# Loads of three key and value tiles for 21 heads, rounds that read all landed tiles first, and longer weight loads, in a single-step attention and mixer kernel

## The chip, the cores and the metric

The kernel runs on one core of a Trainium2 chip. The metric is the time of one execution on the device in microseconds. The engines are named as in the profile: PE (matrix products), PEld (its weight loads), DVE (vector), ACT (activations), POOL, and SP, which here only issues the loads from memory (DMA). The core has sixteen DMA engines, and a load of 128 rows is spread over all of them.

## The reference

One decode step for 4 batch items: layer normalisation modulated by a condition vector, attention of 32 query heads over 8 cached key/value heads of 4096 positions each, an output projection with a gated residual, and a small two-layer mixer on top. All is fp32. Keys and values are 134 MB of the 157 MB that are read.

```python
mod = (silu(c) @ w_mod).reshape(4, 6, 1, 512)
sa, ca, ga, sb, cb, gb = (mod[:, e] for e in range(6))
h = layernorm(x) * (1 + ca) + sa
q = (h @ wq)                                    # 32 heads of 128
s = einsum("bhqd,bhkd->bhqk", q, repeat(k_cache, 4)) * 128 ** -0.5
o = einsum("bhqk,bhkd->bhqd", softmax(s), repeat(v_cache, 4))
x = x + ga * (o.reshape(4, 1, 4096) @ wo)
h = layernorm(x) * (1 + cb) + sb
u = gelu(einsum("bsd,sf->bdf", h, w1) + b1)      # f = 1792
x = x + gb * (einsum("bdf,fs->bds", u, w2) + b2)
```

## The kernel before, in words

The work is cut into NS = 32 heads i (batch item i // 8, key/value head i % 8). A head needs two tiles of 2 MB, its keys K_i and its values V_i, each 128 rows of 16 KB. They pass through a ring of three buffers of two tiles (96 KB of each of the 128 partitions). `load_first` brings K0 and K1 (`kk`), and each `load_pair(i)` brings K_(i+2) and V_i in one load of 4 MB with rows of 32 KB, so that the scores of a head run two rounds ahead of its values. At the start the ring holds weights: wm01 (the modulation's first two slices of `w_mod`) and the two halves of `wq`. In the round i = 1 the three slices wm24 take one ring buffer, and `mod` reads them after round 2. The output weights `wo` have a place of their own (`wo_p`, four tiles of two heads) and come in four loads of 2 MB.

The program writes out by hand the order in which each engine gets its work. A head passes these steps: `scores` (PE into s), `row_max` (DVE), `turn_max` (PE, pm), `col_max` (DVE), `spread_max` (PE, pb), `copy_max` (DVE, nm), `expo` (ACT, p and its row sums l), `turn` (DVE, transposes p in blocks), `sums` (PE, pl), `scale` (DVE), `values` (PE into pv), `copy_v` (DVE, po), `pick` (PE, pt), `copy_o` (DVE, oT), `project` (PE with wo, pa), `add_up` (DVE, acc). The loop over i from 0 to 23 runs, in one round, the scores of head i+2, the picking and projection of head i-1, and the values of head i in two halves. From i = 8 on, `Mixer` puts pieces of the mixer of the batch item before into the rounds (gelu on ACT, expansions on DVE, py on PE). Heads 24 to 31 and the last mixers follow the text `PLAN`, in which each word is a step; LP, LT, LK, LV and LW are its loads. `finish` ends the kernel.

All loads stand in one queue on SP, in program order. A load waits on SP until what is in its place has been read, and every later load waits behind it.

Lines that the prediction speaks of: L176 (pair loads), L181 (wo), L185 and L186 (wm24), L231 (scores), L291 (values), L215 (the products in mod, whose input is wm), L328, L343, L251 and L240 (pt, pa, pb, pm).

Of the kernel before, what the change touches and what calls it, by code (L numbers as in the profile page):

```python
# [15 lines left out]
REP = HQ // HKV  # L16
# [8 lines left out]
NARROW = NS - 3  # L25


@with_exitstack
def adaln_decode(ctx: ExitStack, tc: tile.TileContext, small, x, wmod, wq, kk, kv, vv, wo, out):
# [18 lines left out]
    wm01 = ring.tile([P, 2, 4, D], F32, name="wm01", tag="kv")  # L48
    nc.sync.dma_start(wm01, wmod[0])
# [3 lines left out]
    for k in range(0, 4, 2):  # L53
        t = ring.tile([P, 2, HQ * DH], F32, name=f"wq{k}", tag="kv")
        nc.sync.dma_start(t, wq[k // 2])
        wqt += [t[:, 0], t[:, 1]]
# [34 lines left out]
    wo_p = [wos.tile([P, 2, REP, D], F32, name=f"wo{h}") for h in range(0, HKV, 2)]  # L91
    wo_t = [wo_p[h // 2][:, h % 2] for h in range(HKV)]
# [64 lines left out]
    KT, VT, WM = {}, {}, {}  # L157

    def slots():
        return ring.tile([P, 2, SK], F32, name="kv", tag="kv")  # L160

    def key(t, i):
        KT[i] = t

    def value(t, i):
        VT[i] = t.rearrange("p (j d) -> p j d", d=DH)

    def load_first():
        t = slots()
        nc.sync.dma_start(t, kk)  # L170
        key(t[:, 0], 0)
        key(t[:, 1], 1)

    def load_pair(i):
        t = slots()
        nc.sync.dma_start(t, kv[i])  # L176
        key(t[:, 0], i + 2)
        value(t[:, 1], i)

    def load_wo(h):  # L180
        nc.sync.dma_start(wo_p[h // 2], wo[h // 2])  # L181

    def load_wm24():
        w = ring.tile([P, 3, 4, D], F32, name="wm24", tag="kv")
        nc.sync.dma_start(w[:, 0:2], wmod[1])  # L185
        nc.sync.dma_start(w[:, 2], wmod[2][:, 0])  # L186
        for e in range(3):
            WM[2 + e] = w[:, e]

    def load_wm5():  # L190
        t = slots().rearrange("p s (k n) -> p (s k) n", n=D)
        nc.sync.dma_start(t[:, 0:4], wmod[2][:, 1])
        WM[5] = t[:, 0:4]
        return t[:, 4:6]

    def load_key(t, i):
        nc.sync.dma_start(t, kv[i - 2][:, 0])
        key(t, i)

    def load_v(t, i, cuts):  # L200
        value(t, i)
        src = (kv[i][:, 1] if i < NS - 2 else vv[i - NS + 2]).rearrange("p (j d) -> p j d", d=DH)
        for lo, hi in zip(cuts, cuts[1:]):
            nc.sync.dma_start(VT[i][:, lo:hi], src[:, lo:hi])
# [21 lines left out]
    def scores(i):  # L226
        b, h = divmod(i, HKV)
        S[i] = s = ps_s.tile([P, 1024], F32, name=f"s{i}", tag="s")
        for n in range(2):
            for c in range(4):  # L230
                mm(s[32 * c:32 * c + 32, n * 512:(n + 1) * 512], QT[:, b, h, :],  # L231
                   KT[i][:, (n * 4 + c) * 512:(n * 4 + c + 1) * 512], start=True, stop=True)

# [51 lines left out]
    def values(i, ks):  # L285
        if ks[0] == 0:
            PV[i] = ps_v.tile([P, 4 * DH], F32, name="pv", tag="pv")
        pT = PL[i][0]
        for k in ks:
            q = k % 4  # L290
            mm(PV[i][32 * q:32 * q + 32, :], pT[:, 128 * k:128 * k + 128:4],  # L291
               VT[i][:, 4 * k:4 * k + 4, :].rearrange("p j d -> p (j d)"), start=(k < 4), stop=(k >= 4))

    def values_narrow(i, ks, pv=None):
# [5 lines left out]
        for k in ks:  # L300
            for j in range(4 * k, min(4 * k + 4, top)):
                c = j % 4
                mm(pv[32 * c:32 * c + 32, :], pT[:, j, :], VT[i][:, j, :], start=(k == 0), stop=(j + 4 >= top))  # L303

# [32 lines left out]
    def project(i, pa=None, between=None):  # L337
        b, h = divmod(i, HKV)
        oT = OT[i]
        if pa is None:  # L340
            pa = ps_m.tile([P, D], F32, name="pa", tag="m")
            for g in range(REP):
                mm(pa[32 * g:32 * g + 32, :], oT[:, g:g + 1].to_broadcast([P, 32]), wo_t[h][:, g, :],  # L343
                   start=True, stop=True)
        else:
            for g in range(REP):
                for c in range(4):
                    mm(pa[32 * c:32 * c + 32, :], oT[:, g:g + 1].to_broadcast([P, 32]),  # L348
                       wo_t[h][:, g, c * P:(c + 1) * P], start=(g == 0 and h == HKV - 2),
# [202 lines left out]
    def finish(b, pg, py, hb, wr):  # L552
        uu = ring.tile([P, 16, D], F32, name="uu", tag="kv")
# [35 lines left out]
    def fold_gate(gate, es):  # L589
        for e in es:  # L590
            w = wo_t[HKV - 2 + e // REP][:, e % REP]
# [17 lines left out]
    load_first()  # L609
    load_pair(0)  # L610
    load_wo(0)
# [3 lines left out]
    for step in (turn, sums, scale):  # L615
        step(0)
    mix = None
    for i in range(NS - HKV):
        load_pair(i + 1)
        if i in (1, 3, 5):  # L620
            load_wo(i + 1)
        if i == 1:
            load_wm24()
        scores(i + 2)
        row_max(i + 2)
        if i:
            pick(i - 1)
            copy_o(i - 1)
        turn(i + 1)
        sums(i + 1)  # L630
        scale(i + 1)
        if i:
            project(i - 1)
            add_up(i - 1)
        turn_max(i + 2)
        col_max(i + 2)
        values(i, range(4))
        spread_max(i + 2)
        copy_max(i + 2)
        expo(i + 2)  # L640
        if i and i % HKV == 0:
            mix = Mixer(i // HKV - 1)
        if mix:
            mix.inner(i % HKV)
        values(i, range(4, 8))
        copy_v(i)
        if mix:
            mix.outer(i % HKV)
        if i == 2:
            for t in range(2, 5):  # L650
# [4 lines left out]
                else:  # L655
                    nc.scalar.activation(dst, pm, AF.Copy)
        if i == NS - HKV - 2:
            gate = spread_gate()

    mix, row = Mixer(B - 2), Mixer(B - 1)
    pve = pgx = pc = ep = spare = slot = None
    gates = list(range(2 * REP))
    cuts = {NS - 1: (0, 16, 24, 28, 30, 32), NS - 2: (0, 16, 32)}
# [3 lines left out]
    x LP27 m26 S27 P24 m27 X26 X27 b26 B26 e26 x b27 v25.1 c g t26.1 l25 t26.0 B27 s28 V25 c g L25  # L669
    v26.0 v26.1 S28 x l26 f a25 L26 V26 A25 x m28 p25 LT X28 e27 c a26 P25 t27.0 A26 b28 s29 f B28 p26 e28  # L670
    LK30 t27.1 S29 P26 v27.0 m29 l27 g LK31 T t28.1 X29 LT t28.0 s30 L27 S30 b29 v27.1 B29 e29 l28 m30 V27
    LV28 L28 a27 g X30 t29.1 t29.0 l29 L29 s31 A27 LV29 b30 p27 x B30 S31 c c m31 e30 P27 X31 v28.0 f LT LV30
    b31 v28.1 B31 f e31 LV31 l30 V28 L30 t30.1 l31 L31 a28 t31.1 A28 p28 v29.0 v29.1 t30.0 f P28 V29 v30.0 a29
    v30.1 A29 LW p29 f v30.2 v30.3 t31.0 P29 g V30 Y y a30 A30 p30 E x v31.0 f v31.1 v31.2 v31.3 V31 z31 a31 I A31 j p31
# [3 lines left out]
             "l": sums, "L": scale, "V": copy_v, "a": pick, "A": copy_o, "P": add_up,  # L678
             "LP": load_pair}
# [4 lines left out]
    for step in PLAN.split():  # L684
# [19 lines left out]
        elif op == "LT":  # L704
            slot = slots()
        elif op == "LK":
            load_key(slot[:, i % 2], i)
        elif op == "LV":
            load_v(slot[:, i % 2], i, cuts.get(i, (0, 32)))
        elif op == "LW":  # L710
            spare = load_wm5()
        elif op == "x":
            mix.expand(spare if mix.n == 6 else None)
# [75 lines left out]
```

## Time and profile before

| what | value |
|---|---|
| median of 3 runs (range) | 386.48 us (386.38 to 386.49) |
| span of the profiled execution | 384.7 us |
| mean granted PE clock | 0.883 of full |
| busy: PE, DVE, ACT | 298.7, 198.2, 112.2 us |
| DMA | 157.69 MB, mean 410 GB/s |
| wait of PE at L231 for loads of kv | 37.0 us in 19 waits |

The profiled execution has a span of 384.7 us from its first to its last instruction; the median of the runs is 1.8 us above that. Busy shares are averages over stages: PE is busy for 78% of the span, yet that says nothing on what it waits for. In the rows, a matrix product of fp32 counts twice (16 for the 8 products of one head's scores), and its duration overlaps the next one's: what a group costs is read from its start to the start of the next group.

### The profile page before, as it was taken

What the parts mean: (1) busy time and instruction counts of PE and PEld (TensorE: products, weight loads), DVE (VectorE), ACT (ScalarE), POOL (GpSimd) and SP (SyncE); (2) the same over time, 40 slices, a digit from 0 to 9 for tenths busy, and PEclk for the clock granted to TensorE, in tenths of its full rate; (3) what the DMA queues carried; (4) which work ended last, traced back from release to release, by engine and by line L of the source; (5) the groups of instructions that cost most, each with busy time, mean ns of one, the idle gap of its engine ahead of it and who ended that gap; (6) DMA issues with size and microseconds to landing.
All of it is one profiled execution on the core that took longest, in us unless ns stands there. A gap on an engine that the chain in (4) does not pass through costs nothing.

```text
span 384.7 us, 5604 instructions
## 1 busy us (share of the span) xinstructions
PE 298.7 (78%) x2380; PEld 117.2 (30%) x2380; DVE 198.2 (52%) x407; ACT 112.2 (29%) x144; POOL 7.7 (2%) x33
## 2 busy tenths in 40 slices
PE   0856777866966949979877878788888887999984
PEld 0112122311323313334322222342222343333653
DVE  1130251620451424664866545557665567778757
ACT  1001111121110110212567311124575105657276
POOL 1100000000000000000000000000000000000000
PEclk9989555985695685998999998999999999999999
DMA  8999999999999999999999999999999999999930
GB/s 331 433 433 436 411 453 433 409 432 436 423 441 433 434 436 436 434 436 431 429 425 433 428 433 434 429 433 431 429 434 436 434 436 432 424 417 423 418 122 3
DMA packets 7409, 157.69 MB, mean 410 GB/s; under 512 B 964, under 2 KB 1236, under 8 KB 1496
## 3 DMA queue, kind: packets, MB, share of 16 engines
q1 hardware_dynamic: 7376, 157.33, 95.4%
q8 instruction: 18, 0.29, 0.3%
q14 instruction: 7, 0.06, 0.0%
q10 hardware_dynamic: 8, 0.00, 0.0%
HBM read 157.32 MB, written 0.01 MB: 409 GB/s over the span
## 4 chain that ended last, share of the span: by engine, by line
DMA 60%; PE 29%; DVE 7%; ACT 2%; issue 1%; POOL 0%; SPq 0%; POOLq 0%; DVEq 0%
DMA kv<-in_kv 58%; PE s L231 8%; PE pv L291 7%; PE s L122 2%; PE qs L138 2%; DVE m L236 2%; DVE p L267 2%; DMA sm<-in_small 2%; PE pa L343 2%; PE pt L328 2%; ACT uu L562 1%; PE pb L251 1%; PE pve L303 1%; PE pm L240 1%; PE pgx L348 1%
## 5 line engine op out<-in xcount | busy, mean ns | idle before, releaser
L231 PE MATMUL s<-kv,QT 128*32 128x512 f32 x512 | 75.2, 714 | 38.9 <-DMA kv<-in_kv 37.0
L236 DVE TENSOR_REDUCE m<-s 128x1 f32<-128x1024 f32 x32 | 39.2, 1224 | 96.0 <-PE s L231 95.9
L261 ACT ACTIVATE p<-s,nm 128x1024 f32<-128x1024 f32 x32 | 35.7, 1115 | 180.6 <-DVE nm L256 180.5
L291 PE MATMUL pv<-kv,p 128*32 128x512 f32 x464 | 69.8, 670 | 0.7 <-DMA kv<-in_kv 0.7
L231 PEld LDWEIGHTS s<-kv,QT 128*32 128x32 f32 x512 | 15.8, 123 | 84.0 <-DMA kv<-in_kv 52.5
L328 PEld LDWEIGHTS pt<-g,po 128*128 128x128 f32 x236 | 31.1, 205 | 27.2 <-issue 19.9
L343 PE MATMUL pa<-wo,oT 128*32 128x512 f32 x240 | 34.6, 648 | 4.6 <-DVE oT L335 4.4
L328 PE MATMUL pt<-g,po 128*128 128x4 f32 (+2 forms) x236 | 33.9, 267 | 1.5 <-DVE po L314 1.0
L267 DVE STREAM_TRANSPOSE p<-p 128x1024 f32<-128x1024 f32 x25 | 30.9, 1234 | 0.0
L314 DVE COPY po<-pv 128x512 f32<-128x512 f32 x29 | 20.0, 688 | 16.8 <-PE pv L291 16.7
L245 DVE TENSOR_REDUCE mx<-pm 1x128 f32<-1x512 f32 x32 | 21.3, 669 | 1.1 <-PE pm L240 1.1
L442 DVE TENSOR_SCALAR u<-hb,wr,sm 128x512 f32<-128x512 f32 x40 | 19.9, 541 | 1.9 <-POOL wr L437 1.0
L506 ACT ACTIVATE u<-u 128x1024 f32<-128x1024 f32 x20 | 20.4, 1051 | 1.5 <-DVE u L442 1.4
L361 DVE TENSOR_TENSOR acc<-acc,pa 128x512 f32<-128x512 f32 x26 | 17.8, 686 | 4.3 <-PE pa L343 4.2
L261 ACT ACT_TABLE_LOAD x11 | 14.1, 1283 | 20.3 <-DVE nm L256 20.2
L251 PEld LDWEIGHTS pb<-neg,mx 1*128 1x128 f32 x64 | 10.4, 202 | 28.2 <-DVE mx L245 26.5
L122 PE MATMUL s<-wm,sT 128*4 128x512 f32 x16 | 9.1, 732 | 10.6 <-DVE sT L108 10.6
L506 ACT ACT_TABLE_LOAD x13 | 16.7, 1283 | 0.2
L291 PEld LDWEIGHTS pv<-kv,p 128*32 128x32 f32 x464 | 13.4, 146 | 7.2 <-issue 3.1
L240 PE MATMUL pm<-ident,m 128*1 128x128 f32 x32 | 9.3, 289 | 7.4 <-DVE m L236 3.5
L251 PE MATMUL pb<-neg,mx 1*128 1x1 f32 x64 | 13.1, 271 | 2.1 <-DVE mx L245 2.1
L453 PE MATMUL py<-u,sm 128*32 128x512 f32 x80 | 14.4, 616 | 0.0
(158 smaller groups left out, 214.7 us busy)
## 6 DMA issues: line engine op xcount, KB each, us to landing
kv<-in_kv SPq DMA_DIRECT2D x28, 4096.0 KB, 21.9
wq<-in_wq SPq DMA_DIRECT2D x2, 4096.0 KB, 16.3
wo<-in_wo SPq DMA_DIRECT2D x4, 2048.0 KB
kv<-in_kv SPq DMA_DIRECT2D x4, 2048.0 KB, 20.3
wm<-in_wmod SPq DMA_DIRECT2D x2, 2048.0 KB, 14.8
kv<-in_kk SPq DMA_DIRECT2D x1, 4096.0 KB
kv<-in_vv SPq DMA_DIRECT2D x3, 1024.0 KB
wm<-in_wmod SPq DMA_DIRECT2D x1, 1024.0 KB
```

The source lines that it names most:

```text
L231: mm(s[32 * c:32 * c + 32, n * 512:(n + 1) * 512], QT[:, b, h, :], KT[i][:, (n * 4 + c) * 512:(n * 4 + c + 1) * 512], start=True, stop=True)
L236: dv.tensor_reduce(M[i], S[i], axis=AX.X, op=OP.max)
L245: dv.tensor_reduce(mx, M[i].rearrange("o (c r) -> o r c", c=4).unsqueeze(1).to_broadcast([1, 4, 32, 4]), axis=AX.X, op=OP.max)
L251: mm(pb, M[i].rearrange("o c r -> o (c r)"), neg1, start=True, stop=True)
L261: nc.scalar.activation(p, S[i], AF.Exp, bias=M.pop(i), accum_out=l)
L267: dv.transpose(PL[i][0], PL[i][0])
L291: mm(PV[i][32 * q:32 * q + 32, :], pT[:, 128 * k:128 * k + 128:4], VT[i][:, 4 * k:4 * k + 4, :].rearrange("p j d -> p (j d)"), start=(k < ...
L314: dv.tensor_copy(PV[i], pv)
L328: mm(pt, po[:, c * DH:(c + 1) * DH], sel.unsqueeze(1).to_broadcast([P, m, REP]), start=(c == 0), stop=(c == n - 1))
L343: mm(pa[32 * g:32 * g + 32, :], oT[:, g:g + 1].to_broadcast([P, 32]), wo_t[h][:, g, :], start=True, stop=True)
L442: dv.tensor_scalar(u[:, e, :], hb, wr[:, j:j + 1], b1[:, j:j + 1], op0=OP.mult, op1=OP.add)
L506: nc.scalar.activation(u, u, AF.Gelu_apprx_tanh)
```

## The change

The ring becomes one tile RING of six places. For heads 0 to 20 (NP = 21) the keys and values come in 14 loads of three tiles (6 MB, rows of 48 KB, tensor `kvk`), in turn K_(a+2), V_a, K_(a+3) and V_(a+1), K_(a+4), V_(a+2), for a = 0, 3, .. 18. The prediction calls them T0 to T13. Heads 21 to 27 keep pairs, the rest single tiles. `wo` becomes one tile that is loaded in two loads of 4 MB; wm01 and wm24 lie in its places for later heads (wm24 in heads 4 to 6), no longer in the ring, so kk needs to wait for nothing. `LOADS` lists all loads in order, and `advance` is called after each step that reads a tile: it issues from the front of the list as long as what lies in the place has been read, so the load words leave `PLAN`.

The rounds of heads 0 to 20 become two halves of three tiles each. `first_half(a)` runs scores, values, scores on the tiles of one triple, `second_half(a)` values, scores, values on the next, and picking, projecting and the mixer stand behind. Heads 21 to 23 have rounds of their own (`round_of`). `copy_max` goes from DVE to ACT for heads below 26.

The order of SP's queue from the first keys on, before:

```order
L170 DMA kv<-in_kk 128x8192
L176 DMA kv<-in_kv 128x8192
L181 DMA wo_128<-in_wo 128x4096
L176 DMA kv<-in_kv 128x8192 x2
L181 DMA wo_129<-in_wo 128x4096
L185 DMA wm_337<-in_wmod 128x4096
L186 DMA wm_337<-in_wmod 128x2048
L176 DMA kv<-in_kv 128x8192 x2
```

And after, with the semaphores that a load waits for (PE is a read; DMAHW is an earlier load):

```order
L210 DMA kv<-in_kk 128x8192
L210 DMA kv<-in_kvk 128x12288 [waits DMAHW4_49,DMAHW3_49,PE_49]
L192 DMA wo<-in_wo 128x8192 [waits DMAHW0_49]
L210 DMA kv<-in_kvk 128x12288 [waits DMAHW5_49,PE_49]
L192 DMA wo<-in_wm 128x6144 [waits DMAHW1_49]
L210 DMA kv<-in_kvk 128x12288 [waits DMAHW6_49,DMAHW2_49,PE_49]
L192 DMA wo<-in_wo 128x8192 [waits DMAHW1_49,PE_49]
L210 DMA kv<-in_kvk 128x12288 [waits DMAHW0_49]
```

The second `wo<-in_wo` now waits for PE (the reads of wm24 by mod) and stands ahead of the fourth triple and all that follow, where before wo waited only for an earlier load.

PE around the first run of mod, before (scores of head 4, one round, then mod, which reads wm):

```order
L231 MATMUL s_394<-kv,QT 32x512 x8
L328 MATMUL pt<-g_122,po 128x4 x4
L275 MATMUL pl<-g_122,l 128x4
L343 MATMUL pa<-wo_128,oT 32x512 x4
L240 MATMUL pm<-ident,m 1x128
L291 MATMUL pv<-kv,p 32x512 x4
L251 MATMUL pb<-neg_87,mx 128x1
L291 MATMUL pv<-kv,p 32x512 x4
L215 MATMUL pm_445<-wm_337,sT_134 32x512 x4
L221 MATMUL pc_452<-ym,g_122 32x128 x4
L215 MATMUL pm_458<-wm_337,sT_134 32x512 x4
```

And after (the second half of a = 0, then mod, whose input is now in the place of wo):

```order
L309 MATMUL pv<-kv,p 32x512 x8
L245 MATMUL s_385<-kv,QT 32x512 x8
L309 MATMUL pv<-kv,p 32x512 x8
L255 MATMUL pm<-ident,m 1x128
L350 MATMUL pt<-g_121,po 128x4 x4
L266 MATMUL pb<-neg_87,mx 128x1
L365 MATMUL pa<-wo,oT 32x512 x4
L350 MATMUL pt<-g_121,po 128x4 x4
L365 MATMUL pa<-wo,oT 32x512 x4
L293 MATMUL pl<-g_121,l 128x4
L229 MATMUL pm_449<-wo,sT_129 32x512 x4
L235 MATMUL pc_456<-ym,g_121 32x128 x4
```

The reads of all three tiles now come first, in one run, and mod stands behind the picking and projection of two heads. The first half of a = 3 shows the other kind, on PE right behind mod:

```order
L245 MATMUL s_490<-kv,QT 32x512 x8
L309 MATMUL pv<-kv,p 32x512 x8
L255 MATMUL pm<-ident,m 1x128
L245 MATMUL s_516<-kv,QT 32x512 x8
L266 MATMUL pb<-neg_87,mx 128x1
L350 MATMUL pt<-g_121,po 128x4 x4
L255 MATMUL pm<-ident,m 1x128
L365 MATMUL pa<-wo,oT 32x512 x4
L266 MATMUL pb<-neg_87,mx 128x1
L293 MATMUL pl<-g_121,l 128x4 x2
```

Two scores with a values between them; pm, the turn of the row maxima, is all that stands between the reads.

The diff, cut to its core, with the two halves in full, since they set the order:

```diff
-    ring = ctx.enter_context(tc.tile_pool(name="ring", bufs=3))
+    ring = ctx.enter_context(tc.tile_pool(name="ring", bufs=1))
...
+    RING = ring.tile([P, 6, SK], F32, name="kv")
+    wo_t = wos.tile([P, HKV, REP, D], F32, name="wo")
+    wm01, wm24 = wo_t[:, 0:2], wo_t[:, 4:7]
+    nc.sync.dma_start(wm01, wm0)
...
+    def queue():
+        q = [entry(["K0", "K1"], kk)]
+        for n in range(NT):
+            m = n // 2 * 3
+            names = [f"V{m + 1}", f"K{m + 4}", f"V{m + 2}"] if n % 2 else [f"K{m + 2}", f"V{m}", f"K{m + 3}"]
+            q.append(entry(names, kvk[n]))
...
+        q.insert(2, ("wo", "M0", wo_t[:, 0:4], wo[0]))
+        q.insert(4, ("wo", None, wm24, wm2))
+        q.insert(6, ("wo", "M2", wo_t[:, 4:8], wo[1]))
+        return q
...
+    def advance(name=None):
+        read.add(name)
+        while LOADS:
+            kind, names, *rest = LOADS[0]
+            if kind == "wo":
+                if names not in read:
+                    return
+                nc.sync.dma_start(*rest)
+            else:
+                n, p = len(names), at[0]
+                if any(h not in read for h in held[p:p + n]):
+                    return
...
     def copy_max(i):
         nm = wk.tile([P, 1], F32, name="nm")
-        dv.tensor_copy(nm, M[i])
+        if i < NS - HKV + 2:
+            nc.scalar.activation(nm, M[i], AF.Copy)
+        else:
+            dv.tensor_copy(nm, M[i])
...
+    def first_half(a):
+        do(a + 2, scores, row_max)
+        attend(a)
+        do(a + 2, turn_max, col_max)
+        scores(a + 3)
+        do(a + 2, spread_max, copy_max, expo)
+        row_max(a + 3)
+        do(a, pick, copy_o, begin)
+        do(a + 3, turn_max, col_max)
+        project(a)
+        do(a + 3, spread_max, copy_max)
+        do(a + 2, sums, scale, turn)
+        add_up(a)
+        expo(a + 3)
+        end(a)
+        do(a + 3, sums, scale, turn)
+
+    def second_half(a):
+        attend(a + 1)
+        do(a + 4, scores, row_max)
+        values8(a + 2)
+        do(a + 4, turn_max, col_max)
+        copy_v(a + 2)
+        do(a + 1, pick, copy_o, begin)
+        do(a + 4, spread_max, copy_max, expo)
+        project(a + 1)
+        do(a + 2, pick, copy_o)
+        do(a + 1, add_up, end)
+        begin(a + 2)
+        project(a + 2)
+        do(a + 4, sums, scale, turn)
+        do(a + 2, add_up, end)
...
+    for a in range(0, NP, 3):
+        first_half(a)
+        second_half(a)
+        if a == 0:
             for t in range(2, 5):
                 pm = mod(t)
...
+            advance("M2")
+    for i in range(NP, NS - HKV):
+        round_of(i)
...
-    a23 v24.0 A23 p23 t25.0 P23 F R v24.1 LP25 G s26 t25.1 M H V24 LP26 Q a24 S26 v25.0 N s27 x A24 f p24 g
+    a23 v24.0 A23 p23 t25.0 P23 F R v24.1 G s26 t25.1 M H V24 Q a24 S26 v25.0 N s27 x A24 f p24 g
...
```

`attend` is values of all eight parts and copy_v; `do` runs steps in order; `begin` and `end` are the mixer's pieces around a round. The host packs `kvk`, `wm0`, `wm2`, `wm5` and the two parts of `wo` accordingly.

More of the change, by code (lines that the diff above doesn't have):

```diff
@@ L196, in load_key @@
[L196 to L204, printed above, removed]
+    KT, VT, WM = {}, {}, {2 + e: wm24[:, e] for e in range(3)}
+    held, read = [("Q", 0), ("Q", 0), ("Q", 1), ("Q", 1), None, None], {None, ("Q", 0), ("Q", 1)}
@@ L614, in adaln_decode @@
             step(i)
[L615 to L640, printed above, removed]
-        if i and i % HKV == 0:
[L642 to L649, printed above, removed]
+    for i in range(2):
+        for step in (sums, scale, turn):
+            step(i)
```

161 lines of the change are left out of this document (94 added, 67 removed).

## The prediction

> **What bounds the kernel now.** The page is read first: the transfer rate by slices, the queue table, the chain that ended last.
>
> ```profile
> GB/s 331 433 433 436 411 453 433 409 432 436 423 441 433 434 436 436 434 436 431 429 425 433 428 433 434 429 433 431 429 434 436 434 436 432 424 417 423 418 122 3
> q1 hardware_dynamic: 7376, 157.33, 95.4%
> DMA 60%; PE 29%; DVE 7%; ACT 2%; issue 1%; POOL 0%; SPq 0%; POOLq 0%; DVEq 0%
> ```
>
> From slice 1 to slice 37 the rate lies near 430 GB/s and hardly dips, and 60% of the chain is DMA. The DMA view of the stretch 150 to 300 us and the page's table of issues tell whether the queue ever ran empty.
>
> ```profile
> q1 hardware_dynamic: 2228, 64.62, 99.9%
> kv<-in_kv SPq DMA_DIRECT2D x28, 4096.0 KB, 21.9
> SPq L176 <- PE pv L291: 186.4, 23, 12.3
> ```
>
> The queue holds 99.9% of sixteen engines there. A pair of 4096 KB takes some 9.7 us to move (4.19 MB at 433 GB/s) and lands 21.9 us after its issue: half of that time it stood queued behind another load. SP's waits for PE (third row) cost nothing, since they end long before the queue is empty. So the kernel is bound by its bytes, and a change can win only through the rate, the head or the tail; it loses whatever time the queue stands empty. The end is tight as well, by the chain of waits:
>
> ```profile
> 297.00 21.88 DMA kv<-in_kv
> ...
> 327.22 15.81 DMA kv<-in_kv
> ```
>
> The second row ends with K30's landing, at 343.03; nothing but compute follows it in the chain, to 384.7. That code hardly changes, so the whole tail moves with this landing. The span is 384.7 us and the median of the runs 386.48: 1.8 us lie around the span, and I add my sum to the median.
>
> **Term 1, longer rows.** The bytes stay 157.3 MB. 21 pair loads become 14 triples, four wo loads become two, and the three tiles of wm24 come in one. Two windows compare 32 KB rows (pairs only) with mostly 16 KB rows:
>
> ```profile
> 233.00:318.00 85.00, 69.56 (x561) 29.29 (x554) 53.45 (x106) 28.26 (x33) 1.86 (x4) 1.00 1.00 433
> 330.00:352.00 22.00, 20.74 (x169) 9.04 (x165) 17.61 (x37) 12.88 (x15) 0.00 (x0) 1.00 0.99 426
> ```
>
> Halving the row cost 433/426 = 1.6%, or 0.16 us per 4 MB, for 8 more rows per engine. The triples save 7 x 8 rows per engine (7 x 0.16 = 1.1 us), wo 2 x 0.16, wm about 0.1: **1.5 us** at most. The short window is cut at its edges, so the lower end comes from the landings in the chain above: a pair's at 297.00 + 21.88 = 318.88 and K30's at 343.03, and between them lie two pairs and one 16 KB load, 24.15 us; pairs land 9.7 us apart, which leaves 4.8 for the single load, half a pair, so no cost of a row at all. Between 0 and 1.5 I take **-0.6**, nearer to the landings because they are not cut.
>
> The Trainium skill ("DMA: Bandwidth & Descriptors", Anatomy of one DMA) gives one DMA a fixed part of about 2 us beside its bytes. If each load paid that by itself, the ten loads fewer (7 of kv, 2 of wo, 1 of wm) would by that page save an estimated 20 us. The trace speaks against it: with the queue at 99.9% the fixed part of a load lies under the load before it, and the measurement decides.
>
> **Term 2, the load behind the modulation.** The order of SP shows two new waits. One is the wait of each triple for the reads of the triple before the last (below). The other decides: `wo` for heads 4 to 7 now overwrites wm24, so it waits for the third read of mod (L229 in the new code), and T3 (the fourth triple) and all later loads stand behind it. Here the rows: one round at full clock, with the copy on DVE from the page's groups (its mean in ns is the second number behind the bar), then mod with rows at half clock.
>
> ```profile
> L314 DVE COPY po<-pv 128x512 f32<-128x512 f32 x29 | 20.0, 688 | 16.8 <-PE pv L291 16.7
> ```
>
> ```profile
> 72.81 1.92 PE L231 MATMUL s<-kv,QT 128*32 128x512 f32 x16 [1.08 <-DMA kv<-in_kv]
> 74.67 1.05 PE L328 MATMUL pt<-g,po 128*128 128x4 f32 x8
> ...
> 76.15 1.06 PE L343 MATMUL pa<-wo,oT 128*32 128x512 f32 x8 [0.21 <-DVE oT L335]
> ...
> 78.61 0.38 PE L251 MATMUL pb<-neg,mx 1*128 1x1 f32 x2
> 78.92 1.09 PE L291 MATMUL pv<-kv,p 128*32 128x512 f32 x8
> ```
>
> ```profile
> 82.51 1.47 PE L215 MATMUL pm<-wm,sT 128*32 128x512 f32 x8 [2.49 <-DMA wm<-in_wmod]
> 84.67 0.66 PE L221 MATMUL pc<-ym,g 128*32 128x128 f32 x8 [0.70 <-ACT ym L218]
> 85.73 1.94 PE L215 MATMUL pm<-wm,sT 128*32 128x512 f32 x8 [0.40 <-ACT prep L656]
> ...
> 89.49 1.94 PE L215 MATMUL pm<-wm,sT 128*32 128x512 f32 x8 [0.40 <-ACT prep L656]
> ...
> 94.58 3.64 PE L231 MATMUL s<-kv,QT 128*32 128x512 f32 x16 [1.72 <-DMA kv<-in_kv]
> 98.15 1.87 PE L328 MATMUL pt<-g,po 128*128 128x4 f32 x8
> ...
> 126.82 1.94 PE L291 MATMUL pv<-kv,p 128*32 128x512 f32 x8
> ```
>
> When the bytes come: K4's pair had landed at 72.81. T1 of the new kernel (V1, K4, V2) ends one 2 MB load later in the same stream of bytes, 72.81 + 4.85 = 77.65. Behind it come wm24 (3 MB, 7.3 us) and T2 (14.5): the queue is empty at **99.4** unless wo has been issued. (Check: 94.58, plus 4.85, is 99.4.)
>
> When PE gets there: T0 ends 24.2 us (T1 and a wo load) before T1, at 53.4, and its half takes PE some 14 us (8.3 for the reads and 6 for the rest, as worked out next), to 68. PE then idles about 10 us, so it starts at half clock. Four windows (the last numbers of a row are the granted clock, the DMA share and GB/s) show what such a gap does, and when the clock returns:
>
> ```profile
> 112.50:118.80 6.30, 0.00 (x0) 0.00 (x0) 0.66 (x1) 0.32 (x2) 0.00 (x0) 0.87 0.98 421
> 119.00:130.70 11.70, 11.70 (x53) 4.07 (x54) 4.04 (x7) 1.13 (x2) 0.00 (x0) 0.50 1.00 427
> 171.80:175.20 3.40, 2.97 (x16) 0.60 (x16) 0.02 (x1) 0.00 (x0) 0.00 (x0) 0.50 0.96 414
> 175.20:178.60 3.40, 3.03 (x27) 1.59 (x27) 2.92 (x5) 0.00 (x0) 0.00 (x0) 1.00 0.96 410
> ```
>
> After 6.3 idle us the clock stood at 0.50 for 11.7 us of mixed work; in one stretch of nothing but score matmuls it came back after 3.4 us. The new order puts values, scores, values back to back, so I take 5 us at half clock. Scores and values cost 3.6 + 2 x 3.7 = 11.0 us at half clock (94.58 to 98.15; values two groups of about 1.9) and 1.9 + 2 x 2.1 = 6.0 at full: 5 + 6.0 x 6.0/11.0 = 8.3 us. Then pm 0.2, pt 0.9, pb 0.3, a wait of 0.6 for copy_v (0.69 on DVE) and copy_o, pa 1.0, pt 0.9 and copy_o 0.2, pa 1.0, pl 0.3: 5.3 us. Then mod to its third read: 8.9 us in the trace (82.51 to 91.43, nearly all at half clock), and at full clock 2 x 2.6 + 1.1 = 6.3, with 2.6 = 1.1 + 0.7 (ACT) + 0.4 + 0.4 (ACT). At full clock SP issues wo at 77.65 + 8.3 + 5.3 + 6.3 = **97.6**; where the clock falls during the sparse rest, pa and pt double too (+1.5) and mod takes 9: **101.8**.
>
> What the issue needs before 99.4: the head and the end of the run show it.
>
> ```profile
> 0.72 0.39 SPq L49 DMA_DIRECT2D wm<-in_wmod  x1
> ```
>
> ```profile
> 1.00:2.00 1.00, 0.00 (x0) 0.00 (x0) 0.49 (x2) 1.00 (x1) 0.29 (x1) 1.00 1.11 213
> ...
> 366.00:367.00 1.00, 1.00 (x46) 0.97 (x40) 0.88 (x3) 0.69 (x1) 0.00 (x0) 1.00 0.92 354
> ...
> 369.00:370.00 1.00, 0.87 (x40) 0.60 (x28) 0.16 (x1) 0.06 (x1) 0.00 (x0) 1.00 0.22 82
> ```
>
> The first load, issued at 0.72, moves bytes from between 1 and 2 us: 1 us of lead. And the sixteen engines do not end together: at the last load the share falls from 0.92 to 0.22 within some 3 us. At 99 us I take a spread of 2, so the first engines are empty at 97.2 and the last at 99. An issue at 97.6 gives bytes at 98.6: the early engines lose 1.4 us, the late ones nothing. What the end loses lies between 0 and 1.4; I take **+1.1**, nearer to the early engines, because no row tells which engine will be the last at the end, and an early one of now may be.
>
> **Term 3, steady state: nothing.** A triple must be read before the next one has moved (14.5 us), less 1 us of lead and up to 3 of spread: 10.5 us after landing. Starting cold it is read after 8.3 (above; a first half with two scores and one values is the same). That leaves 2 us, so I cost it at zero; if PE came more than 2 us late into a triple, each such load would lose the excess. copy_max, a copy of 128x1, goes from DVE to ACT, where expo stood waiting for it before as well: nothing, and without that cover a fraction of a us per head, inside the slack of a triple. In the head kk is issued some 16 us earlier, but the queue holds the two wq loads at that time: nothing. Sum: -0.6 + 1.1 = **+0.5, 387.0 us**.
>
> **The rivals.** (1) *wo comes late*: the clock falls during the rest of the round and mod, issue at 101.8, bytes at 102.8, 3.8 to 5.6 us empty, say 5: -0.6 + 5 = +4.4, **390.9**. For it: mod ran at half clock in the trace. Against: there PE had waited 2.49 us just before, here it comes from dense work. It decides from an issue at about 98.3 on, where the loss of the early engines passes 1.9 us. (2) *The clock falls before every triple*: PE now works in bursts and waits once per 14.5 us; a whole half at half clock needs 3 x 3.65 + 2 x 1.87 + 1.9 + 1.5 = about 18 us of PE, so it would end 3.5 us late, and its successor's loads be issued about 1.5 us too late (2 us of slack against 3.5). With a third of 14 triples so, 5 x 1.5: +7 - 0.6 = **392.9**. The Trainium skill ("TensorE: Matmul & The Clock Gate", HAM oscillation) tells of just this: a wait beyond some 3.4 us before each burst makes every burst start cold. The rows 112.50 to 130.70 agree that it happens here; that it drains the queue no row shows. (3) *Only the rows count*: wo is issued in time (PE at full clock from 3 us on, mod without waits) and rows pay the windows' price, -1.5: **385.0**. (4) *Nothing*: rows are cut into the same pieces as before and wo comes in time: **386.5**.
>
> **How the numbers follow.** Forecast 387.0 with 0.40 (its own range 386.2 to 388.0); rival 1 0.23, rival 2 0.12, rival 3 0.15, rival 4 0.10. 0.2% of 386.48 is 0.8 us, about what a measurement can tell from no change: 385.7 to 387.25. Faster: rival 3 and a rest of rival 4 that gains a little, 0.18. Same: most of the forecast and of rival 4, 0.37. Slower: a third of the forecast, rivals 1 and 2, 0.45. The range goes from 385.2 (rows pay nearly in full) to 391.6 (rival 1 with its upper price); rival 2 and the edge of rival 3 stay outside.
>
> **What would show it.** Right: the issue of the second wo near 97 to 98 us, the rate by slices at 430 to 436 with at most one dip about slice 10, PE's clock lower than before in many slices, triples landing 14.5 us apart, K30 near 343.5. Rival 1: a slice near 100 us well under 400 GB/s, and mod's rows at 1.94. Rival 2: dips all along, and loads that land under 20 us after issue. Rival 3: triples 14.45 us apart and no dip. It would be wrong in a way not listed if the tail, from K30's landing to the end (41.6 us), changed its length.

## The result, and the profile after

The changed kernel takes **402.69 us** (399.77 to 403.77 in 4 runs) where the kernel before takes 386.49: a ratio of 1.0385, with a 95% interval of 1.031 to 1.046. The forecast was 387.0, with a range from 385.2 to 391.6. The ratios, here and below, leave disturbed runs out; medians are over all runs. The profiled execution has a span of 402.0 us (before 384.7) and a mean granted PE clock of 0.812 (0.883).

The page of the changed kernel: clock and transfer rate by slices, the queue's share, the chain that ended last.

```profile
PEclk9969766596855896785986788889687677999999
GB/s 323 443 437 417 466 419 458 398 465 346 450 416 455 403 460 406 457 412 445 426 427 406 432 372 315 446 427 414 445 427 429 424 359 276 409 430 421 325 3 2
q1 hardware_dynamic: 5936, 157.33, 92.0%
PE 49%; DMA 34%; ACT 8%; DVE 6%; issue 1%; SPq 1%; POOL 0%; POOLq 0%; ACTq 0%
```

The chain was 60% DMA before and is 49% PE now, and the rate dips in slices 9, 23 to 24 and 32 to 33. Windows of the changed kernel at the dips and at the end (the last three numbers of a row: granted clock, DMA share, GB/s):

```profile
95.00:100.00 5.00, 3.39 (x20) 0.60 (x24) 0.29 (x1) 0.60 (x1) 0.00 (x0) 0.50 0.79 295
240.00:245.00 5.00, 4.85 (x44) 1.99 (x36) 3.40 (x6) 2.09 (x3) 0.00 (x0) 1.00 0.54 167
...
315.00:340.00 25.00, 22.09 (x151) 10.21 (x151) 11.80 (x26) 4.10 (x7) 1.30 (x3) 0.71 0.81 327
...
379.00:402.00 23.00, 15.78 (x362) 11.04 (x354) 15.11 (x45) 12.79 (x17) 0.76 (x2) 0.98 0.05 19
```

And the end before, where the last bytes of values come at about 367:

```profile
367.00:384.70 17.70, 11.35 (x236) 7.31 (x228) 11.22 (x32) 12.10 (x17) 0.76 (x2) 0.96 0.09 35
```

So the bytes end some 12 us later (the last values land at about 367.3 before and at 378.9 after), because the queue ran empty three times: behind wo, before T12 (issued at 242.6) and before the last two pairs (issued at 322.6 and 336.1). Against the 433 GB/s of a full queue the three windows lack 1.6, 3.1 and 6.1 us of bytes, 10.8 of the 11.6; a little more than their empty shares say (about 1, 2.3 and 4.8 us). After the bytes PE needs 23 us where it needed 17.5. The empty stretches and the long tail look like four causes. The waits of PE for loads between 185 and 285 us, in which the mixer runs, say that one lies behind all but the first. Before (who waited for whom: us in total, times, longest):

```profile
PE s L231 <- DMA kv<-in_kv: 15.7, 10, 2.5
```

After:

```profile
PE pl L293 <- ACT nm L272: 2.6, 3, 2.1
...
PE pv L309 <- DMA kv<-in_kvk: 0.2, 1, 0.2
```

Before, PE reached every tile early and waited for it, 15.7 of 100 us. After, it waits for data once, 0.2 us: from about 185 us on **PE is late**, and at 240 us and between 315 and 340 us **the queue waits for PE**. The prediction had it the other way round. Rounds 21 to 23 show how PE gets later still. PE's timeline of round 22, after:

```profile
302.65 3.34 PE L245 MATMUL s<-kv,QT 128*32 128x512 f32 x16
305.81 1.89 PE L309 MATMUL pv<-kv,p 128*32 128x512 f32 x16
307.63 0.27 PE L255 MATMUL pm<-ident,m 128*1 128x128 f32 x1
308.53 1.05 PE L350 MATMUL pt<-g,po 128*128 128x4 f32 x8 [0.63 <-DVE po L336]
309.52 0.38 PE L266 MATMUL pb<-neg,mx 1*128 1x1 f32 x2
309.84 1.06 PE L365 MATMUL pa<-wo,oT 128*32 128x512 f32 x8
312.67 0.59 PE L293 MATMUL pl<-g,l 128*128 128x4 f32 x2 [1.77 <-ACT p L279]
313.19 1.94 PE L475 MATMUL py<-u,sm 128*32 128x512 f32 x8
315.94 0.65 PE L388 MATMUL pc<-yw,g 128*32 128x128 f32 x8 [0.81 <-DVE yw L544]
316.52 2.08 PE L606 MATMUL pgb<-prep,ident 128*128 128x128 f32 x8
318.53 2.23 PE L245 MATMUL s<-kv,QT 128*32 128x512 f32 x16
```

The same stretch before, from the scores of head 24 to those of head 25:

```profile
289.74 1.92 PE L231 MATMUL s<-kv,QT 128*32 128x512 f32 x16 [1.62 <-DMA kv<-in_kv]
...
292.51 0.36 PE L275 MATMUL pl<-g,l 128*128 128x4 f32 x2
...
300.07 1.92 PE L231 MATMUL s<-kv,QT 128*32 128x512 f32 x16
```

`round_of(i)` runs the scores of head i+2 and the values of head i without a break, then picks and projects head i, and takes head i+2 through exponentials, sums, scale and turn within the same round. It takes 15.9 us here, and the round before took 10.3. Two things differ. The waits inside the round sum to 3.2 us, before to 1.2. And the mean granted clock is 0.71 in this round, where it was 1.00 before (third number from the end): the scores, `py` and `pgb` take nearly twice as long. The round after the change, then before:

```profile
302.65:318.53 15.88, 12.67 (x81) 5.41 (x73) 6.85 (x12) 3.80 (x6) 0.00 (x0) 0.71 1.01 434
```

```profile
289.74:300.07 10.33, 9.14 (x77) 3.95 (x78) 5.65 (x10) 3.74 (x5) 0.00 (x0) 1.00 1.02 439
```

`pl`, the row sums, now belongs to the head whose scores the same round has made, so PE stands 1.77 us for ACT's exponentials; before, it belonged to the head of the round before and waited for nothing.

### The profile page after: what moved, and what is told of

Its sections match the earlier page's. It is cut to its first block, busy times and chain, and to the rows that moved or that the text cites. A ratio compares the mean times of both kernels' runs of the same rounds, so it can differ in the third digit from the quotient of the medians.

```text
span 402.0 us, 5589 instructions
## 1 busy us (share of the span) xinstructions
PE 309.3 (77%) x2380; PEld 127.6 (32%) x2380; DVE 196.0 (49%) x381; ACT 114.1 (28%) x168; POOL 7.7 (2%) x33
## 4 chain that ended last, share of the span: by engine, by line
PE 49%; DMA 34%; ACT 8%; DVE 6%; issue 1%; SPq 1%; POOL 0%; POOLq 0%; ACTq 0%
DMA kv<-in_kvk 26%; PE pv L309 14%; PE s L245 13%; DMA kv<-in_kk 9%; PE pt L350 4%; PE pa L365 4%; PE py L475 3%; ACT p L279 2%; ACT L279 2%; ACT u L528 1%; ACT kv L584 1%; PE pl L293 1%; PE pb L266 1%; DVE mx L260 1%; DVE po L336 1%
## 5 line engine op out<-in xcount | busy, mean ns | idle before, releaser
L272 ACT ACTIVATE nm<-pb 128x1 f32<-128x1 f32 x26 | 4.4, 169 | 165.9 <-PE pb L266 165.8
L365 PE MATMUL pa<-wo,oT 128*32 128x512 f32 x240 | 40.1, 721 | 4.2 <-DVE oT L357 2.4
L309 PEld LDWEIGHTS pv<-kv,p 128*32 128x32 f32 x464 | 17.6, 145 | 60.8 <-issue 31.8
L350 PE MATMUL pt<-g,po 128*128 128x4 f32 (+2 forms) x236 | 32.7, 262 | 3.9 <-ACT nm L272 2.0
L350 PEld LDWEIGHTS pt<-g,po 128*128 128x128 f32 x236 | 30.7, 202 | 12.0 <-ACT nm L272 4.7
L245 PEld LDWEIGHTS s<-kv,QT 128*32 128x32 f32 x512 | 17.5, 131 | 46.2 <-issue 39.4
L293 PE MATMUL pl<-g,l 128*128 128x4 f32 x64 | 15.3, 309 | 13.4 <-ACT p L279 9.6
L293 PEld LDWEIGHTS pl<-g,l 128*128 128x128 f32 x64 | 12.6, 245 | 31.7 <-ACT p L279 14.0
L475 PE MATMUL py<-u,sm 128*32 128x512 f32 x80 | 21.0, 881 | 1.3 <-ACT u L528 1.2
L298 DVE RECIPROCAL rl<-pl 128x4 f32<-128x4 f32 x32 | 5.6, 175 | 27.4 <-PE pl L293 27.3
L123 PE MATMUL s<-wo,sT 128*4 128x512 f32 x16 | 9.6, 767 | 10.3 <-DVE sT L109 10.3
## 6 DMA issues: line engine op xcount, KB each, us to landing
kv<-in_kv SPq DMA_DIRECT2D x7, 4096.0 KB, 17.7
```

What stands on the lines that cost most here:

```text
L293: mm(pl, PL[i][1].to_broadcast([P, P]), eight, start=True, stop=True)
L350: mm(pt, po[:, c * DH:(c + 1) * DH], sel.unsqueeze(1).to_broadcast([P, m, REP]), start=(c == 0), stop=(c == n - 1))
L475: mm(py[32 * q:32 * q + 32, :], w2[:, j:j + 1].to_broadcast([P, 32]), u[:, e, :], start=(j < 4), stop=(j >= NF - 4))
```

## The experiments

Each kernel is the changed one with the edit shown; the kernel before ran beside it, at 386.45 to 386.52 us. The theories at the start: CLOCK (PE is late because its clock is halved), WAITS (it is late through the copy that went to ACT), RING (six places leave triples too little slack), and from e5 on HANDOVER (rounds 21 to 23 and their passing to PLAN make it late).

**What the clock and the copy on ACT do.** e1 undoes the move of copy_max alone.

```diff
-        if i < NS - HKV + 2:
-            nc.scalar.activation(nm, M[i], AF.Copy)
-        else:
-            dv.tensor_copy(nm, M[i])
+        dv.tensor_copy(nm, M[i])
```

> copy_max back on DVE for all heads; all else as in the changed kernel. Theory CLOCK (the light products now stand in one stretch behind the reads, PE's clock falls there, PE gets late, and with it the loads and the tail): 399 to 402 us, clock still near 0.82. Theory WAITS (PE loses the time in order, behind ACT, where copy_max now stands behind gelu and table loads): PE's waits for nm at L272 vanish, about 6 us, so 393 to 397. Theory RING (two places of three tiles leave too little slack, the empty queue is the first cause): no change, 400 to 403.

Measured: 406.44 us (ratio 1.0496, 1.0429 to 1.0564). The copy on ACT costs nothing; WAITS falls.

e2 adds products of 128x512 that are thrown away, `warm(a)`, at two places in each half from a = 3 on:

```diff
+    def warm(a):
+        if a:
+            pd = ps_v.tile([P, D], F32, name="pd", tag="pv")
+            for c in range(4):
+                mm(pd[32 * c:32 * c + 32, :], g32, wo_t[:, 0, 0, :], start=True, stop=True)
```

> The changed kernel with extra work that is thrown away: twice in each half from a = 3 on, four products of 128x512 on fixed data go into the idle pv bank between the light products, about 1.9 us of PE per half at full clock (26 us of PE in all). Theory CLOCK: the clock stays up (mean above 0.90) and the time falls to 388 to 394 in spite of more work. Theory WAITS: PE waits less but ends no earlier, 400 to 406. Theory RING: 402 to 410, since PE reads later.

Measured: 403.71 us (1.0416, 1.0338 to 1.0495), mean clock 0.879. The windows of e2:

```profile
185.00:285.00 100.00, 92.70 (x744) 39.87 (x736) 58.40 (x106) 37.66 (x52) 2.07 (x5) 0.97 1.00 429
235.00:245.00 10.00, 9.10 (x70) 3.72 (x70) 5.82 (x10) 4.04 (x7) 0.00 (x0) 0.96 1.00 415
315.00:340.00 25.00, 21.84 (x149) 8.77 (x141) 14.15 (x29) 5.96 (x8) 1.30 (x3) 0.78 0.81 328
```

The clock stays up (0.97) and the empty stretch before T12 is gone, so that stretch does come from the clock; but the one at 315 to 340 us stays (share 0.81), and the time with it. e7 puts `warm` into rounds 21 to 23 as well (twice behind the projection in rounds 21 and 22, once at the end of each round).

> The changed kernel with the thrown-away products of the warm run, and three sets more in each of rounds 21 to 23, so that the clock stays up there too. CLOCK: 391 to 396, queue no longer empty at 310 to 340 us. HANDOVER (the waits for ACT and DVE make the rounds long, not the clock): 399 to 406, no better than the warm run's 403.7.

Measured: 400.86 us (1.0367, 1.0277 to 1.0457). The share at 315 to 340 us is 0.99, but PE still needs 23.9 us after the last bytes, as in e2: the queue is full there, and the end is late all the same. These two don't price the clock itself, since the thrown-away products use PE time of their own (24 groups of about 1.1 us in e2).

**Triples or rounds.** e3 keeps triples and ring but has the rounds, and copy_max, of before:

```diff
-    for a in range(0, NP, 3):
-        first_half(a)
-        second_half(a)
...
+    for i in range(NS - HKV):
+        scores(i + 2)
+        row_max(i + 2)
...
+        values(i, range(4))
...
+        values(i, range(4, 8))
+        copy_v(i)
```

> Loads, ring and copy of the changed kernel's queue (triples, long weight loads), but the rounds of before (scores of i+2, picking of i-1, values of i in two halves; copy_max on DVE). Theory CLOCK: light and dense work alternate again, clock 0.87 or more, 386 to 391. Theory WAITS: the same, 386 to 391. Theory RING: a triple is given back only after one and a half rounds, the queue empties at each, 395 or more with dips all along.

Measured: 398.99 us (1.031, 1.0237 to 1.0383). Here PE waits for data again (14.3 us for keys between 185 and 285, in 3 waits), and the rate in that stretch is 411 GB/s, where the kernel before moves 431 to 433. That fits RING: rounds of one head hold a triple's places too long.

e4 is the counterpart, pairs in three places with the new rounds:

```diff
-            q.append(entry(names, kvk[n]))
-        for i in range(NP, NS - 4):
-            q.append(entry([f"K{i + 2}", f"V{i}"], kv[i - NP]))
+        for i in range(NS - 4):
+            q.append(entry([f"K{i + 2}", f"V{i}"], kv[i]))
```

> The rounds of the changed kernel (first_half, second_half, round_of, copy_max on ACT), but pairs in three places for all heads, as before; weight loads stay long, wo's second load stands one pair later. Theory CLOCK and theory WAITS: PE is late all the same, 395 to 402, clock near 0.82. Theory RING: 386 to 389, the queue never empty.

Measured: 398.12 us (1.029, 1.0226 to 1.0355). So the new order of the rounds loses 11 to 12 us without any triple. Its queue never stood empty before 315 us, and PE waited for data 0.2 us in all between 185 and 285: PE is late here too.

e8 has neither: the rounds of before and pairs, with the new ring, the weights in fewer, longer loads, kk at once.

> One part alone: the new ring, queue and long weight loads (wo in two, wm24 in one, in wo's places, kk at once) with pairs and the rounds of before. All theories: 386 to 387; over 388 if the second wo load behind mod, one pair later here than in the changed kernel, still lets the queue run empty, by what the windows near 100 us show.

Measured: 386.58 us (0.9982, 0.9948 to 1.0016): no difference. The ring, the list of loads and the long weight loads are free, and bring nothing.

**Rounds 21 to 23.** e5 gives them the order of before:

```diff
-        round_of(i)
+        scores(i + 2)
+        row_max(i + 2)
+        if i > NP:
+            pick(i - 1)
+            copy_o(i - 1)
+            do(i + 1, turn, sums, scale)
+            project(i - 1)
+            add_up(i - 1)
+        turn_max(i + 2)
+        col_max(i + 2)
+        values(i, range(4))
+        do(i + 2, spread_max, copy_max, expo)
+        begin(i)
+        values(i, range(4, 8))
+        copy_v(i)
+        end(i)
```

> The changed kernel, but rounds 21 to 23 in the order of before (picking and projection of i-1, turn of i+1, values in two halves) in place of round_of. New theory HANDOVER (round_of carries each head through expo, sums and turn within its own round, PE waits for ACT and DVE there, comes late to PLAN, the loads of pairs 24 to 27 are issued late and the tail starts late): the empty queue between 310 and 340 us goes (5 us) and the tail from the last data to the end shrinks from 23 to about 18, so 391 to 395. Theory CLOCK: PE is late long before, 399 or more.

Measured: 393.71 us (1.0156, 1.0094 to 1.0219), 9.0 less. So HANDOVER is shown as the largest single loss. Window 315 to 340 of e5, beside the share of 0.81 above:

```profile
315.00:340.00 25.00, 21.64 (x172) 9.23 (x166) 17.05 (x38) 12.35 (x14) 1.30 (x3) 0.93 1.01 435
```

e6 is e4 with the same edit.

> Pairs in three places, halves of the changed kernel for heads 0 to 20, rounds 21 to 23 in the order of before. HANDOVER: 386 to 389, since the run with pairs had an empty queue only from 315 us on. CLOCK: 394 or more, the halves themselves make PE late.

Measured: 390.82 us (1.0067, 1.0025 to 1.0108), 7.3 less than e4 by the medians and 2.2%, some 8.6 us, by the ratios. So `round_of` costs 7 to 9 us, with triples or pairs.

Which of its moves? e9 does a head's sums, scale and turn one round later and leaves pick and project in their round; e10 does the opposite.

```diff
         do(i + 2, scores, row_max)
+        if i > NP:
+            do(i + 1, sums, scale, turn)
...
-            do(i + 2, sums, scale, turn)
```

```diff
         do(i + 2, scores, row_max)
+        if i > NP:
+            do(i - 1, pick, copy_o, project, add_up)
...
-        if i < NS - HKV - 1:
-            do(i, pick, copy_o)
```

> The changed kernel, but in rounds 21 to 23 a head's row sums, scale and turn are done one round later, behind the next head's scores and row maximum; pick and projection stay in the head's own round. Undoing the whole order of the last rounds gave 393.7 us. EXPO-WAIT (PE waits inside a round for the exponentials of the head whose scores it has just made, about 1.8 us at a time in the trace, and this makes rounds 21 to 23 late for the last pair loads): 393 to 396 us, the queue's empty time between 320 and 340 us falls from about 4.5 us to under 2. PICK-WAIT (the wait is in the pick and projection, for the turned weights' copies): no gain, 400 us or more.

> The changed kernel, but in rounds 21 to 23 pick and projection of a head are done one round later, behind the next head's scores; its row sums, scale and turn stay in its own round. EXPO-WAIT: no gain, 399 us or more. PICK-WAIT: 393 to 396 us and the queue's empty time between 320 and 340 us under 2 us.

Measured: e9 399.26 us (1.032, 1.028 to 1.0361), e10 406.89 (1.0516, 1.0483 to 1.0549). In e9 the queue is full between 315 and 340:

```profile
315.00:340.00 25.00, 21.46 (x147) 9.21 (x148) 16.80 (x35) 6.55 (x8) 1.31 (x3) 0.80 1.00 431
```

In e10 the wait for the exponentials has grown, because pick and projection no longer lie under it. Its timeline of PE in round 21:

```profile
296.25 0.38 PE L266 MATMUL pb<-neg,mx 1*128 1x1 f32 x2 [1.21 <-DVE mx L260]
299.41 0.39 PE L293 MATMUL pl<-g,l 128*128 128x4 f32 x2 [2.78 <-ACT p L279]
```

PICK-WAIT falls. EXPO-WAIT is right on the mechanism and on the queue. On the size the time says 3.4 us by the medians, of 9.0, and the intervals of e9 and of the changed kernel still overlap. The trace says more for it. PE's scores of heads 23 to 26 in e9, that is the start of rounds 21, 22 and 23 and of PLAN:

```profile
294.79 1.99 PE L245 MATMUL s<-kv,QT 128*32 128x512 f32 x16
302.38 1.90 PE L245 MATMUL s<-kv,QT 128*32 128x512 f32 x16
312.92 1.92 PE L245 MATMUL s<-kv,QT 128*32 128x512 f32 x16
327.07 3.64 PE L245 MATMUL s<-kv,QT 128*32 128x512 f32 x16
```

Round 22 takes 10.5 us, at a granted clock of 1.00, as before the change. The three rounds take 32.3 us, against 40.6 in the changed kernel and 30.7 in e5. So in these executions this one move brings 8.3 of the 9.9 us that the whole order of before brings inside the rounds. But e9 came to round 21 3.0 us later than the changed kernel (294.8 against 291.8), in an execution whose queue had run empty for about 4 us behind wo (below). Whether its other executions started late as well is not on record.

**The second wo, and T12.** e11 is e5 with one number changed:

```diff
-        q.insert(6, ("wo", "M2", wo_t[:, 4:8], wo[1]))
+        q.insert(7, ("wo", "M2", wo_t[:, 4:8], wo[1]))
```

> The changed kernel with the last rounds in the order of before (393.7 us), and the second load of wo one triple later in the queue. QUEUE (what is left over before is made of two stretches with an empty queue, behind wo at 95 to 100 us and before T12 at 240 to 245 us): the first stretch is filled, and the time falls by its 1 to 2 us, to 391.5 to 392.7 us. CLOCK (what is left is PE at half clock, whatever the queue does): within 0.6 us of 393.7.

Measured: 389.52 us (1.0079, 1.0055 to 1.0103): 4.2 less than e5 by the medians, 0.8% by the ratios; no run of e11 (388.70 to 391.79) is as slow as one of e5 (392.50 to 394.48). Its window behind the place of wo, and the price on PE, its wait for wo between 105 and 185 us:

```profile
95.00:100.00 5.00, 2.63 (x32) 0.76 (x36) 0.29 (x1) 1.47 (x3) 0.00 (x0) 1.00 1.07 462
```

```profile
PE pa L365 <- DMA wo<-in_wo: 1.2, 1, 1.2
```

QUEUE is right that the stretch is filled, but the gain is more than the 1 to 2 us expected. The profiled executions, 393.77 and 389.32 us, show where it lies. The windows of e5, then of e11:

```profile
95.00:100.00 5.00, 2.84 (x36) 0.80 (x40) 0.29 (x1) 1.27 (x3) 0.00 (x0) 1.00 0.78 275
240.00:245.00 5.00, 4.86 (x42) 2.24 (x38) 3.34 (x5) 2.51 (x4) 0.00 (x0) 1.00 0.54 167
```

```profile
235.00:240.00 5.00, 4.92 (x43) 2.07 (x35) 3.69 (x5) 1.01 (x2) 0.00 (x0) 1.00 0.84 324
240.00:245.00 5.00, 3.82 (x27) 1.72 (x31) 3.48 (x7) 3.02 (x6) 0.00 (x0) 0.90 0.90 374
```

The stretch behind wo lacked 1.8 us of bytes in e5, as QUEUE said. The one before T12 shrank too, from 3.1 us to 1.9. The last values land 3.6 us earlier (369.3 against 372.9), and PE then needs 18.0 us where it needed 19.1. Why these two shrank as well was not tested. And the stretch behind wo is not the same in every execution: up to this issue e9 has the same instructions as the changed kernel, and it issued wo 3.6 us later. SP's timeline of the changed kernel, then of e9:

```profile
97.04 0.33 SPq L192 DMA_DIRECT2D wo<-in_wo  x1
```

```profile
100.67 0.33 SPq L192 DMA_DIRECT2D wo<-in_wo  x1
```

The windows say why, of the changed kernel and then of e9 (granted clock third from the end):

```profile
90.00:95.00 5.00, 2.75 (x32) 0.52 (x24) 1.53 (x2) 1.75 (x4) 0.00 (x0) 0.89 1.03 444
```

```profile
90.00:95.00 5.00, 3.89 (x26) 0.99 (x26) 1.89 (x3) 0.87 (x2) 0.00 (x0) 0.50 1.03 444
```

In e9 the queue was then empty for about 4 us (a share of 0.59 between 95 and 105 us). So the empty stretch behind this load runs from about 1 to 4 us by where the clock happens to step.

e14 makes the same edit in the changed kernel itself.

> The changed kernel as it is, with the second load of wo one triple later and nothing else. ADDS (the late wo costs its 4 us whatever comes behind it): 398 to 399.5 us. HIDDEN (in the changed kernel the last rounds are bound by PE, so that data that come 4 us earlier wait there): 401 us or more.

Measured: 401.56 us (1.0367, 1.034 to 1.0394), the changed kernel's 1.0385 within both intervals. That is what HIDDEN said: bytes that come earlier wait for a PE that is late anyway.

e12 is e5 with `warm` only for a = 9, 12 and 15; e13 is e11 with it.

> The changed kernel with the last rounds in the order of before (393.7 us), and extra products that are thrown away in the halves of the triples 9, 12 and 15 only, ahead of T12's issue. CLOCK (T12 is issued late because PE is at half clock in these halves): the empty stretch at 240 to 245 us is gone, 390 to 391.5 us. WORK (the halves are late by their waits and their order, whatever the clock): the stretch stays, 393 us or more.

> The changed kernel with the last rounds of before, the second load of wo one triple later (389.5 us so far), and the thrown-away products in the halves of the triples 9, 12 and 15. SLACK (what is left of the loss, some 3 us, is the late issue of T12, and half of that is the clock in the mixer's halves): the stretch with an empty queue at 235 to 245 us is gone, 387.3 to 388.5 us. TRANSFER (the triples themselves move slower, or the end is later): no gain, 389 to 390 us.

Measured: e12 392.73 us (1.0145, 1.0107 to 1.0183), e13 389.35 (1.0075, 1.0052 to 1.0098): neither differs from its base. In e12 the stretch before T12 is gone, as CLOCK said, and the time has not fallen. e13's queue was never empty, so its time is the cleanest look at what is left. Its rows: the chain's last load (T13: issue, and us to its landing), then PE's timeline.

```profile
247.94 22.34 DMA kv<-in_kvk
```

```profile
270.32 3.65 PE L309 MATMUL pv<-kv,p 128*32 128x512 f32 x16 [2.42 <-DMA kv<-in_kvk]
...
288.44 1.89 PE L245 MATMUL s<-kv,QT 128*32 128x512 f32 x16
...
350.74 1.92 PE L245 MATMUL s<-kv,QT 128*32 128x512 f32 x16
```

PE starts on T13 as it lands (270.3), and needs 18.1 us for this half (at a mean granted clock of 0.70), values, scores, values and two heads' mixer steps, where a triple brings 14.5 us of bytes. Head 23's scores start at 288.4; before, they started at 280.05. Rounds 21 to 23 and PLAN make up for a part of the 8 us: the last scores come 2.2 us late (350.74; 348.54 before), and the span ends 3.1 us later, though the last values land at 367.6, about as before. The slack theory falls here: it is PE's lateness, not the queue.

e15 is e11 with triples for heads 0 to 11 only, so that most rounds with mixer pieces (they begin with head 8) have pairs and the order of before:

```diff
-NT = 14
+NT = 8
```

> Triples for the first 12 heads only (T0 to T7), then pairs and rounds as before, with the second load of wo one triple later. SLACK (a ring of two triples has too little slack for the rounds in which the mixer runs, heads 8 to 23): no empty queue behind T3, 386.2 to 387.6 us. ROWS (if longer rows gain anything, it shows here, where nothing is late): under 386 us. TRANSFER: 388.5 us or more.

Measured: 387.08 us (1.002, 0.999 to 1.0049). Its PE waits for data again between 185 and 285 us:

```profile
PE s L245 <- DMA kv<-in_kv: 8.5, 5, 3.5
```

The last scores start at 348.29 and the last values land at 367.2, both about as before. No version beats the kernel before; e8 and e15 equal it.

| kernel | us | step |
|---|---|---|
| changed | 402.69 | |
| e5: rounds 21 to 23 as before | 393.71 | -9.0 |
| e11: and wo one triple later | 389.52 | -4.2 |
| e15: and triples only up to head 11, rounds as before from 12 on | 387.08 | -2.4 |
| before | 386.5 | -0.6, within the interval |

The steps hold in this order only: wo alone brings nothing measurable (e14).

## Why the prediction was wrong

**What bounds the kernel** was right for the kernel before, and the failure is that it was carried over to the changed one.

**Term 1, longer rows, -0.6.** Triples land 14.50 us apart, against 14.53 for three halves of a pair, some 0.4 us over 14 loads; no kernel shows it in its time (e8 0.9982, e15 1.002, both intervals with 1 in them). Rival 3, the rows' full price, falls.

**Term 2, the second wo.** The mechanism and the place were right. In the profiled execution the time was right as well (97.04 against 97.6), in part by luck: the reads took 6.7 us and not 8.3, and mod 7.5 and not 6.3, its third product at half clock. The size is not one number. The stretch was empty for about 1 us in this execution, as forecast, and for about 4 us in e9, near rival 1, and the clock during mod decides it, as that rival said. What it is worth in time depends on the rest: moving the load away gained 4.2 us where the last rounds were those of before (e11), more than the stretch itself held, and nothing measurable in the changed kernel (e14).

**Term 3, "steady state: nothing", is the step that failed**, in two places.
First, "a triple must be read before the next one has moved": the reads do fit as long as PE is early: T5 to T9 were issued 6.3 to 8.1 us after the landing of the triple whose places they take (8.3 predicted). But I costed only the reads of a half and took for granted that PE has finished the half before when a triple lands. With the mixer the whole half counts. In the changed kernel the half on T9 ran from 216.6 to 236.9:

```profile
216.63 3.65 PE L309 MATMUL pv<-kv,p 128*32 128x512 f32 x16
...
236.87 1.90 PE L245 MATMUL s<-kv,QT 128*32 128x512 f32 x16
```

That is 20.3 us at a mean clock of 0.74, against 14.5 of supply; T10 had landed at 227.9 and had to wait for PE until 236.9, and T12, which takes T10's places, was issued at 242.6. PE's lateness adds up in such halves: T10 to T13 are issued 9.5, 10.6, 14.7 and 11.9 us after such a landing, where 10.5 were allowed. The clause "if PE came more than 2 us late into a triple, each such load would lose the excess" named the event and gave it no price.
Second, `round_of` and the handover to PLAN had no term at all. That was the largest part, 7 to 9 us (e5, e6), and most of it inside the rounds is the place of the row sums (e9).

**The tail.** "That code hardly changes" is true of PLAN, and the conclusion that it "moves with K30's landing" is not: it grew from 41.6 to 47.6 us, because PE came into it late. The prediction listed this as a way to be wrong.

**Rival 2**, the clock falling before every triple, came nearest in time (392.9), and 18 us was its price for a half. Its signs are there only in part: the rate dips in three places and not all along, and the last seven pairs land a median 17.7 us after issue. The clock does fall: with PE busy 88% of the stretch it is 0.80; the same stretch before, 79% busy, had 0.97. After, then before:

```profile
185.00:240.00 55.00, 48.63 (x324) 18.93 (x316) 29.27 (x50) 22.12 (x27) 0.76 (x2) 0.80 0.99 422
```

```profile
185.00:240.00 55.00, 43.68 (x340) 15.61 (x339) 34.30 (x66) 22.43 (x26) 0.00 (x0) 0.97 1.00 431
```

At half clock the same products take longer, so a part of the 88% is the fall itself. But holding the clock up with added work gains nothing (e2, e12, e13), so the clock is a part of why a half takes 18 to 20 us, and thrown-away work is not the lever. How much a full clock would bring if it came at no PE time stays open. An estimate from e2's rows: its half on T9 took 18.5 us, with 2.1 of thrown-away products and one group of values at half clock (3.55 in place of 1.9), so about 14.7 us without both, no less than a triple's 14.5. Rival 4, no change, is out by the result.

## What to carry to other kernels

In a kernel bound by its queue, PE's waits for loads are its margin: count the whole work between two landings, not only the reads, and compare with what the stage before waited (15.7 us in 100 here). When loads get longer, a stage's work comes in lumps, and each lump must fit under one load at the clock that this stage really has. When an order changes, cost the place where it hands over to the next one; and judge a filled gap in the queue by the last instruction, since three gaps that were filled here (e7, e12, e14) gained nothing measurable while PE was late.

## What the runs showed of the hardware

- The clock steps down in stretches where PE is busy nine tenths of the time (0.80 above), not only after a long wait (PE's longest between 185 and 240 us was 2.1 us); in the same code it stood at 0.89 or at 0.50 between 90 and 95 us in two executions (changed kernel and e9).
- A spread goes with it: the changed kernel's four runs lie over 4 us, and the longer ones have the lower clock (0.812 at 403.77 us, 0.828 at 399.77), while those of before beside them lie within 0.4. The Trainium skill ("TensorE: Matmul & The Clock Gate", What's actually happening) says that the window by which the clock is set runs freely, so that the same kernel warms up at varying points, and puts the cost of this warming up under 1% of a typical span. The variation agrees with these runs. On the size: one such stretch in the middle of the kernel moved the issue of wo by 3.6 us here, 0.9% of the span by itself.
- Rows of 48 KB move no faster than rows of 32 KB by any time that could be measured: 14.50 us for a triple, 1.5 times 9.7 for a pair.
